# Row maxima out of PSUM by one ScalarE copy, split by ScalarE and GpSimd; bias and residual added by GpSimd

## The chip, the cores and the metric

The kernel runs on one core of one Trainium2 chip. The metric is the device time of one execution in microseconds (us); lower is better. A core has five engines that work side by side, each through its own instruction queue in order: TensorE (PE, with its weight loads shown as PEld), VectorE (DVE), ScalarE (ACT), GpSimd (POOL) and SyncE (SP), which here issues the DMAs. SBUF is the working memory with 128 partitions, PSUM holds the results of TensorE.

## The reference

For x of 2048 tokens and 640 channels:

```python
xn = layernorm(x)
qkv = xn @ wqkv                                  # 32 heads of 20 channels
scores = q @ k.T * 20 ** -0.5                    # each query sees itself and the 255 tokens before it
p = softmax(where(mask, scores, -1e9))
s = (p @ v, heads joined) @ wo
h = relu(xn @ w1 + b1) ** 2                      # 640 -> 1536
g = silu(h @ w2 + b2)                            # 1536 -> 640
return x + s * g
```

## The kernel before

All in 32-bit floats, but TensorE gets most operands as a sum of a rounded high part and a low part (the difference), and adds the products of the parts. Work on the two halves of the 128 partitions (64 rows each) is issued in pairs.

The kernel has three stages. A start normalises x, transposes it and computes values and the first queries and keys. The main loop runs over 16 pairs of heads with 16 blocks of 128 tokens each, one block a step (`for s in range(steps)`, L1165), and fills TensorE in between with the other query and key projections (`qkps`) and the dense branch (`hps`, `yps`). The end transposes the attention's output (`otp`), multiplies it by `wo` (`wops`), and puts gate and residual to it. The order of instructions on every engine is written out by the program: it keeps a planner's clock in `clock[0]`, `fill(upto)` emits filling matmuls until the clock has come to the given time, and `later(wait, fn)` puts a function on a list that `soon` runs once the clock has gone `wait` further. `post` collects DMAs, which `post_all` issues on SP in the order posted.

The softmax needs the maximum of each row before the exponential, but the exponential is taken on transposed scores, where rows lie along the columns. So there are two passes over the scores. At step s, `scores` (L479) computes a block of rows into `sps` (L487), and `maxima` (L491) lets VectorE add the mask and take the row maxima (L495), each into its column of the tile `mt`. After every fourth block, at s % 4 == 0, `max_rows` (L497) transposes `mt` on TensorE (L502), which gives eight rows (2 heads, 4 blocks) of 128 maxima. They go into columns 384 to 447 of the tile that the transposed scores of the same step use. `rest` has ScalarE write the negated high part into `mrow` (L510), and `lows` has VectorE write the low part (L513), both reading the maxima in PSUM. Then four small DMAs (posted in L517, issued in L614) put the rows into the query tile `qs`, as two further rows of the contraction beside its 60. Nine steps after a block of rows, `scores_t` (L527) computes the transposed scores `stps` (L534) for a block of keys, from keys and queries with these two rows, so that they come out with the maxima subtracted. `exps` (L538) has ScalarE take the exponential (L540) into `p32`, and GpSimd zero what is outside the window (L541, L543). A step later ScalarE makes the half-precision high part (`high`, L548), VectorE then the low part (`low`, L554). `values` (L561) multiplies both with the values, `normed` (L587) copies the result out of PSUM (L590), adds its parts and divides on GpSimd (L596 to L600).

The block of keys at step s needs the maxima of three blocks of rows, the last of which is block s - 7 of the pair; the rows posted at a step with s % 4 == 0 are first read three steps later.

What matters for order:

- `pair_tile` (L524) comes from a pool of one buffer: the next step's L534 can write only when all readers of the tile are done, the exponential L540 and, in every fourth step, the readers of the maxima.
- In the loop body, `max_rows` emits the transposes after `scores_t`, then `maxima` follows; `rest` is put off by 1.0 of the planner's clock, and `lows` by another 0.5 from there. So the exponential, and work of other jobs, comes before L510 on ScalarE.
- `mt` is one tile: 32 * (g % 2) picks the columns of a group of four blocks, so successive groups write to different columns, and their rows in PSUM and in `mrow` lie on partitions 0 to 7 and 32 to 39 in turn.
- `mrow` is one buffer, read by the DMAs.

In the end stage, `transposes(u)` (L1080) handles 256 tokens: VectorE adds the bias `b2t` to the dense branch's output `yb` (L1082), then comes the transposition of the attention's output with its split (`split`: ScalarE L108, VectorE L109). ScalarE applies silu (L1112). For each of two token blocks and two halves of the columns, 15 matmuls make `wops`, and `evac` (L1132) lets VectorE multiply it with the gate (L1133) and add the residual (L1134), before the result is stored.

Of the kernel before, what the change touches and what calls it, by code (L numbers as in the profile page):

```python
# [9 lines left out]
F32 = mybir.dt.float32  # L10
F32R = mybir.dt.float32r
BF16 = mybir.dt.bfloat16
F16 = mybir.dt.float16
AF = mybir.ActivationFunctionType
ALU = mybir.AluOpType

P = 128
S = 2048
D = 640
# [10 lines left out]
KR = NPART * DH  # L30
HP = P // 2
# [22 lines left out]
def f32(ap):  # L54
    return ap.bitcast(F32)
# [3 lines left out]
def attn_mlp_kernel(ctx: ExitStack, tc, x, wqkv, wo, w1, b1, w2, b2, out):  # L59
    nc = tc.nc  # L60
    PSUM = bass.MemoryType.PSUM
    const = ctx.enter_context(tc.tile_pool(name="const", bufs=1))
# [26 lines left out]
    ident = const.tile([P, P], F32, name="ident")  # L89
# [4 lines left out]

    nc.gpsimd.affine_select(mask[:, 0:P], mask[:, 0:P], pattern=[[1, P]], compare_op=ALU.is_gt, fill=NEG, base=0, channel_multiplier=-1)
    nc.gpsimd.affine_select(mask[:, 2 * P:], mask[:, 2 * P:], pattern=[[-1, P]], compare_op=ALU.is_ge, fill=NEG, base=0, channel_multiplier=1)
    mt = const.tile([P, P], F32, name="mt")
    nc.gpsimd.memset(mt, 0.0)
    ones = const.tile([2, P], F32, name="ones")
    nc.gpsimd.memset(ones, 1.0)  # L100
    ebias = const.tile([P, 1], F32, name="ebias")
# [389 lines left out]
    def maxima(p, q, ss, nk):  # L491
        for hh in range(2):
            junk = at2.tile([P, 3 * P], BF16, tag="junk", bufs=1, name="junk")
            m = 32 * (q // 4 % 2) + 4 * hh + q % 4
            nc.vector.tensor_tensor_reduce(out=junk[:, :nk], in0=ss[hh][:, :nk], in1=mask[:, 3 * P - nk:], scale=1.0, scalar=-3.0e38, op0=ALU.add, op1=ALU.max, accum_out=mt[:, m:m + 1])  # L495

    def max_rows(p, g, tps):  # L497
        i = p % 2

        def one(j):  # L500
            r = slice(j * HP, (j + 1) * HP)
            nc.tensor.transpose(tps[:, j, 3 * P:3 * P + HP], mt[r, :], ident[r, r])  # L502
        both(lambda: one(0), lambda: one(1), COST[P])

        def rest():
            m = slice(32 * (g % 2), 32 * (g % 2) + 8)
            mrow = at2.tile([40, 2, P], F32R, tag="mrow", bufs=1, name="mrow")[m]
            hi, lo = (mrow[:, a, :].rearrange("m (j n) -> m j n", j=2) for a in range(2))
            src = tps[m, :, 3 * P:3 * P + HP]
            nc.scalar.activation(hi, src, AF.Copy, scale=-1.0)  # L510

            def lows():
                nc.vector.scalar_tensor_tensor(lo, src, -1.0, f32(hi), ALU.mult, ALU.subtract)  # L513
                for hh in range(2):
                    for a in range(2):
                        o = hh * HP + KR + a
                        post(f32(qs[i])[o:o + 1, g * 512:(g + 1) * 512].rearrange("r (q n) -> r q n", q=4), f32(mrow)[4 * hh:4 * hh + 4, a, :])  # L517
            later(0.5, lows)
        return rest

    pts = {}
# [87 lines left out]
    def post(dst, src):  # L609
        posts.append((dst, src))  # L610
# [14 lines left out]
    def later(wait, fn):  # L625
        tasks.append((clock[0] + wait, len(tasks), fn))
# [444 lines left out]
    def out_filler(wo_part):  # L1071
        oT, xts = {}, {}
        b2t = wgt.tile([P, D], F32, tag="wgkl", name="b2t")
        nc.sync.dma_start(b2t, b2.partition_broadcast(P))

        def load_res(t):
            xts[t] = wgt.tile([P, D], F32, tag="wgkh", name="xres")
            nc.sync.dma_start(xts[t], x[t * P:(t + 1) * P, :])

        def transposes(u):  # L1080
            ob, yb = ld[u]
            nc.vector.tensor_add(yb, yb, b2t.unsqueeze(1).to_broadcast([P, 2, D]))  # L1082
            big = bigp.tile([P, KC * BT], F32R, tag="big", name=f"oT_{u}")
            oT[u] = big.rearrange("p (s c n) -> p s c n", s=2, c=KC)
            for c0 in range(0, KC, 2):
                cs = range(c0, min(c0 + 2, KC))
                flush(mark() - 2)
                if state[2] < 10 ** 6:
                    ps = mm_bank([P, len(cs), MT], "otp")
                else:  # L1090
                    ps = pat.tile([P, len(cs), MT], F32, tag="s", name="otp")
                for c in cs:
                    for t in range(2):
                        nc.tensor.transpose(ps[:, c - c0, t * P:(t + 1) * P], ob[:, t, c * P:(c + 1) * P], ident)
                        yield 0.12

                def evac(ps=ps, c0=c0, n=len(cs)):
                    split(oT[u][:, 0, c0:c0 + n], oT[u][:, 1, c0:c0 + n], ps)
                pending.append(evac)

        load_res(0)
        for u in range(2 * NB):
            while u not in ld:
                load(u)
                if u not in ld:
                    yield None
            load(u + 1)
            if u not in oT:
                yield from transposes(u)
            flush()  # L1110
            yb = ld[u][1]
            nc.scalar.activation(yb, yb, AF.Silu)  # L1112
            for t2 in range(2):
                t = 2 * u + t2
                xt = xts.pop(t)
                res = wgt.tile([P, D], F32, tag="wgqh", name="res")
                for nh in range(2):
                    if t2 and not nh and u + 1 in ld:
                        yield from transposes(u + 1)
                    sl = slice(nh * HALF, (nh + 1) * HALF)  # L1120
                    ps = mm_bank([P, HALF], "wops")
                    mms = []
                    for c in range(KC):
                        for op, wp in ((0, 0), (0, 1), (1, 0)):
                            mms.append((oT[u][:, op, c, t2 * P:(t2 + 1) * P], wo_part(wp, c)[:, sl]))
                    yield from mm_group(ps, mms, 0.133)
                    if nh == 0 and t + 1 < NT:
                        load_res(t + 1)
                    load(u + 1)
                    load(u + 2)  # L1130

                    def evac(ps=ps, sl=sl, t2=t2, nh=nh, res=res, xt=xt, t=t, yb=yb):  # L1132
                        nc.vector.tensor_mul(res[:, sl], ps, yb[:, t2, sl])  # L1133
                        nc.vector.tensor_add(res[:, sl], res[:, sl], xt[:, sl])  # L1134
                        if t == NT - 1:
                            post(out[t * P:(t + 1) * P, sl], res[:, sl])
                        elif nh:
                            post(out[t * P:(t + 1) * P, :], res)
                    pending.append(evac)
# [18 lines left out]
    with tc.manual_schedule(engines={E_.PE, E_.Activation, E_.DVE, E_.Pool, E_.SP}):  # L1158
# [6 lines left out]
        for s in range(steps):  # L1165
            state[2] = s
            vload[0] = 0.2 * (s % 4 == 0) + 0.5 * (s % 4 == 3)
            post_all()
            issue(RATE)
            a, b, c, d, e = (at_step(s - lag) for lag in (0, LAG, LAG + 1, LAG + 2, LAG + 3))  # L1170
            if a:
                p, q = a
                if q == 0:
                    ensure_bulk(loads)
                if s == 2:
                    ones_rows(1)
                if q == 2 and p < NP - 1:
                    loads = [bulk_dma(0.7, *l) for l in pair_loads(p + 1, 0)]
                if q == LAG and p < NP - 1:
                    loads += [bulk_dma(0.7, *l) for l in pair_loads(p + 1, 1)]  # L1180
                if q == LAG + 4 and p < NP - 1:
                    load_v(p + 1)
            rows = None
            if a:
                sc = scores(p, q)
            if b:
                stp = scores_t(*b)
            if s % 4 == 0 and 0 < s <= NP * NT:
                rows = max_rows((s - 1) // NT, (s - 1) % NT // 4, stp[0] if b else pair_tile())
            if a:  # L1190
                maxima(*a, *sc)
            if rows:
                later(1.0, rows)
            if norm:
                norm.pop()()
            if b:
                exs[b] = (exps(*b, *stp), stp[1])
            fill((s + EARLY_FILL) * pace)
            drain(urgent)
            if summed:  # L1200
                norm.append(normed(*summed.popleft()))
            post_all()
            issue(RATE)
            if d:
                low(*d)
            flush()
            tick()
            if c:
                high(*c, *exs.pop(c))
            while lastn:  # L1210
                lastn.pop()()
            if e and e[1] % 2:
                fill((s + 1) * pace - 24 * COST[61])
                values(*e)
            else:
                fill((s + 1) * pace)
# [37 lines left out]
```

## Time and profile before

| | |
|---|---|
| median of 3 runs | 985.9 us (984.94 to 987.88) |
| the profiled execution, its time | 987.44 us |
| its span, first to last instruction | 985.4 us |
| mean granted TensorE clock | 0.983 |
| first and last transposes of maxima (L502) | 126.8 and 849.7 us |
| transposes of maxima / copies L510 / subtractions L513 | 128 / 64 / 64 |
| bias additions L1082 on VectorE | 8, 1485 ns each |
| residual additions L1134 on VectorE | 32, 492 ns each |

A row of the profile's timeline has the start, the duration, the engine, the line of the kernel, the operation, what is written from what, the tile's partitions and columns, and the number of instructions merged in the row; in brackets the idle time of the engine before it, with the engine and line that ended it. A row of the waits has the waiting engine and line, what it waited for, the total in us, how often, and the longest. A row of the groups has the count, the busy total in us and the mean of one in ns, and then the engine's idle time before them. All names are the program's own.

### The profile page before, as it was taken

The page shows a single profiled execution, that of the slowest core. Times are in us where ns is not written, and L with a number is a line of the kernel's source. Part 1 is how long each engine was busy: PE and PEld are TensorE (multiplying, and loading weights), DVE is VectorE, ACT ScalarE, POOL GpSimd, SP SyncE. Part 2 cuts the span into 40 slices and gives each one's busy share as a digit, 9 for nine tenths or more (in the row PEclk, how much of TensorE's full clock was granted, in tenths as well). Part 3 has the DMA queues.
Part 4 walks back from the last instruction along what each step waited for, and adds up shares of the span by engine and source line. Part 5 has one row for each costly group of instructions (what it writes and reads, how often), then busy time and mean ns, then how long its engine had stood idle before and what let it go on. Part 6 is the DMA issues. An engine that isn't in the chain of part 4 may idle for free.

```text
span 985.4 us, 35528 instructions
## 1 busy us (share of the span) xinstructions
PE 900.9 (91%) x14368; PEld 862.4 (88%) x14368; DVE 752.1 (76%) x1869; ACT 637.1 (65%) x1080; POOL 501.8 (51%) x798
## 2 busy tenths in 40 slices
PE   9999998999898899899999789898899899898898
PEld 8999998888888899798898788798889789897887
DVE  6864478788999878678888788788688778755664
ACT  5433247686788878678878778767757767852221
POOL 5010015454567767667757657657656676850000
PEclk9999999999999999999999999999999999999999
DMA  7996787578784543452553354463454273065663
GB/s 264 313 382 248 216 279 253 189 227 251 218 258 120 163 120 93 131 153 65 164 145 93 83 149 124 115 194 100 124 156 125 49 230 107 11 201 190 246 242 108
DMA packets 106876, 169.95 MB, mean 172 GB/s; under 512 B 42840, under 2 KB 60376, under 8 KB 104152
## 3 DMA queue, kind: packets, MB, share of 16 engines
q1 hardware_dynamic: 106712, 167.68, 54.3%
q8 instruction: 113, 1.85, 0.8%
q14 instruction: 51, 0.42, 0.2%
HBM read 96.15 MB, written 70.91 MB: 170 GB/s over the span
## 4 chain that ended last, share of the span: by engine, by line
PE 61%; ACT 13%; DVE 11%; DMA 8%; issue 5%; SPq 1%; DVEq 0%; ACTq 0%; POOL 0%; POOLq 0%
PE yps L477 11%; PE hps L477 8%; PE ops L477 8%; PE wops L649 7%; PE vps L228 7%; PE qkps L477 6%; PE stps L534 5%; ACT ph L548 4%; PE sps L487 3%; ACT p L540 3%; PE qkps L205 3%; DVE junk L495 2%; DVE mrow L513 2%; DVE pl L554 2%; ACT relu L959 2%
## 5 line engine op out<-in xcount | busy, mean ns | idle before, releaser
L495 DVE CUSTOM_DVE_ANT_0 junk<-sps,mask 128x384 bf16<-128x384 f32 (+2 forms) x512 | 271.3, 530 | 97.8 <-PE sps L487 47.0
L540 ACT ACTIVATE p<-stps,ebias 128x768 f32<-128x768 f32 (+2 forms) x256 | 219.9, 859 | 158.0 <-PE stps L534 126.9
L541 POOL TENSOR_SCALAR_AFFINE_SELECT p<-p 128x256 f32<-128x256 f32 x256 | 165.1, 645 | 269.8 <-ACT p L540 227.1
L477 PE MATMUL yps<-w,hh 64*128 64x320 f32 x1536 | 260.4, 319 | 6.1 <-DVE sq L964 5.8
L554 DVE TENSOR_TENSOR pl<-p,ph 128x768 f16<-128x768 f32 (+2 forms) x256 | 248.4, 971 | 1.9 <-ACT ph L548 1.5
L477 PE MATMUL hps<-xb,w 64*128 64x256 f32 x2520 | 236.9, 289 | 0.1
L477 PEld LDWEIGHTS hps<-xb,w 64*128 64x128 f32 x2520 | 224.9, 191 | 0.3 <-DVE sq L964 0.3
L477 PEld LDWEIGHTS yps<-w,hh 64*128 64x128 f32 x1536 | 201.3, 189 | 9.5 <-DVE sq L964 8.9
L477 PE MATMUL ops<-vp,ph 64*128 64x61 bf16 x2880 | 205.5, 191 | 0.1
L548 ACT ACTIVATE ph<-p 128x768 f16<-128x768 f32 (+2 forms) x256 | 203.6, 795 | 1.8 <-POOL p L543 1.8
L477 PE MATMUL ops<-vp,pl 64*128 64x61 bf16 x2880 | 203.0, 190 | 0.0
L477 PE MATMUL yps<-w,hl 64*128 64x320 f32 x768 | 192.6, 316 | 0.0
L477 PEld LDWEIGHTS <-ph 64*128 64x128 f16 x2880 | 178.0, 95 | 3.8 <-PE ops L477 0.3
L477 PEld LDWEIGHTS <-pl 64*128 64x128 f16 x2880 | 179.1, 95 | 0.0
L534 PE MATMUL stps<-qs,ks 62*128 62x384 f32 (+2 forms) x512 | 107.9, 360 | 60.7 <-DVE mrow L513 60.3
L543 POOL TENSOR_SCALAR_AFFINE_SELECT p<-p 128x256 f32<-128x256 f32 x224 | 136.0, 607 | 0.0
L534 PEld LDWEIGHTS stps<-qs,ks 62*128 62x128 f32 x512 | 62.8, 190 | 78.1 <-DVE mrow L513 77.8
L477 PEld LDWEIGHTS yps<-w,hl 64*128 64x128 f32 x768 | 122.7, 188 | 0.0
L487 PE MATMUL sps<-ks,qs 60*128 60x384 f32 (+2 forms) x512 | 115.7, 357 | 0.8 <-DVE mt L495 0.7
L477 PE MATMUL qkps<-xT,wgkh 64*128 64x512 f32 x320 | 103.9, 402 | 0.0
L477 PE MATMUL qkps<-xT,wgqh 64*128 64x512 f32 x320 | 103.2, 398 | 0.0
L965 POOL TENSOR_TENSOR hl<-sq,hh 128x256 fp32r<-128x256 f32 x96 | 83.6, 877 | 17.0 <-DVE sq L964 14.2
(109 smaller groups left out, 1622.3 us busy)
## 6 DMA issues: line engine op xcount, KB each, us to landing
ks<-k_d SPq DMA_DIRECT2D x64, 240.0 KB
qs<-q_d SPq DMA_DIRECT2D x64, 240.0 KB
xb<-xs SPq DMA_DIRECT2D x12, 1280.0 KB
xs<-xT SPq DMA_DIRECT2D x8, 1280.0 KB
y<-ysb SPq DMA_DIRECT2D x32, 320.0 KB
k_d<-shm SPq DMA_DIRECT2D x19, 512.0 KB
q_d<-shm SPq DMA_DIRECT2D x19, 512.0 KB
v_d<-vt SPq DMA_DIRECT2D x8, 976.0 KB
```

The lines of the kernel that those rows point to most:

```text
L228: nc.tensor.matmul(ps, xT[xp][b][:, c * BT + t * P: c * BT + (t + 1) * P], wv[wp][:, c, nh * HALF:(nh + 1) * HALF], start=first and m == 0 ...
L477: return nc.tensor.matmul(out, a[r], b_[r], skip_group_check=True, **kw)
L487: nc.tensor.matmul(ss[hh][:, :nk], qs[i][o, q * P:(q + 1) * P], ks[i][o, k0 * P:k0 * P + nk], start=True, stop=True)
L495: nc.vector.tensor_tensor_reduce(out=junk[:, :nk], in0=ss[hh][:, :nk], in1=mask[:, 3 * P - nk:], scale=1.0, scalar=-3.0e38, op0=ALU.add, o ...
L534: nc.tensor.matmul(tps[:, hh, :n], ks[i][o, kb * P:(kb + 1) * P], qs[i][o, kb * P:kb * P + n], start=True, stop=True)
L540: nc.scalar.activation(p32[:, :, :n], tps[:, :, :n], AF.Exp, scale=SCALE, bias=ebias)
L541: nc.gpsimd.affine_select(p32[:, :, 0:P], p32[:, :, 0:P], pattern=[[0, 2], [1, P]], compare_op=ALU.is_ge, fill=0.0, base=0, channel_multip ...
L543: nc.gpsimd.affine_select(p32[:, :, 2 * P:], p32[:, :, 2 * P:], pattern=[[0, 2], [-1, P]], compare_op=ALU.is_gt, fill=0.0, base=0, channel ...
L548: nc.scalar.activation(ph[:, :, :n], p32[:, :, :n], AF.Copy)
L554: nc.vector.tensor_sub(pl[:, :, :n], p32[:, :, :n], ph[:, :, :n])
L649: nc.tensor.matmul(ps, a, b_, start=j == 0, stop=j == n - 1)
L965: nc.gpsimd.tensor_sub(hh[1][:, sl], sq, f32(hh[0][:, sl]))
```

## The change

The single tile for the maxima becomes two tiles of 64 columns, used by successive groups. The transposes therefore give 64 rows, of which the first eight hold the maxima, always on partitions 0 to 7. One ScalarE copy takes the negated maxima out of PSUM into `row` in SBUF. From there ScalarE writes the high part into `mrow`, and GpSimd subtracts to get the low part. All this is no longer put off by the planner's clock: it is emitted right behind the step's exponential, and the exponential now stands ahead of `norm.pop()`. In the end stage, the additions of bias and residual move from VectorE to GpSimd.

```diff
-    mt = const.tile([P, P], F32, name="mt")
-    nc.gpsimd.memset(mt, 0.0)
+    mts = [const.tile([P, HP], F32, name=f"mt{j}") for j in range(2)]
+    for t_ in mts:
+        nc.gpsimd.memset(t_, 0.0)
...
     def maxima(p, q, ss, nk):
         for hh in range(2):
             junk = at2.tile([P, 3 * P], BF16, tag="junk", bufs=1, name="junk")
-            m = 32 * (q // 4 % 2) + 4 * hh + q % 4
-            nc.vector.tensor_tensor_reduce(out=junk[:, :nk], in0=ss[hh][:, :nk], in1=mask[:, 3 * P - nk:], scale=1.0, scalar=-3.0e38, op0=ALU.add, op1=ALU.max, accum_out=mt[:, m:m + 1])
+            m = 4 * hh + q % 4
+            nc.vector.tensor_tensor_reduce(out=junk[:, :nk], in0=ss[hh][:, :nk], in1=mask[:, 3 * P - nk:], scale=1.0, scalar=-3.0e38, op0=ALU.add, op1=ALU.max, accum_out=mts[q // 4 % 2][:, m:m + 1])
 
     def max_rows(p, g, tps):
         i = p % 2
 
         def one(j):
             r = slice(j * HP, (j + 1) * HP)
-            nc.tensor.transpose(tps[:, j, 3 * P:3 * P + HP], mt[r, :], ident[r, r])
+            nc.tensor.transpose(tps[:HP, j, 3 * P:3 * P + HP], mts[g % 2][r, :], ident[r, r])
         both(lambda: one(0), lambda: one(1), COST[P])
 
         def rest():
-            m = slice(32 * (g % 2), 32 * (g % 2) + 8)
-            mrow = at2.tile([40, 2, P], F32R, tag="mrow", bufs=1, name="mrow")[m]
-            hi, lo = (mrow[:, a, :].rearrange("m (j n) -> m j n", j=2) for a in range(2))
-            src = tps[m, :, 3 * P:3 * P + HP]
-            nc.scalar.activation(hi, src, AF.Copy, scale=-1.0)
-
-            def lows():
-                nc.vector.scalar_tensor_tensor(lo, src, -1.0, f32(hi), ALU.mult, ALU.subtract)
-                for hh in range(2):
-                    for a in range(2):
-                        o = hh * HP + KR + a
-                        post(f32(qs[i])[o:o + 1, g * 512:(g + 1) * 512].rearrange("r (q n) -> r q n", q=4), f32(mrow)[4 * hh:4 * hh + 4, a, :])
-            later(0.5, lows)
+            row = at2.tile([8, P], F32, tag="row", bufs=1, name="row")
+            mrow = at2.tile([8, 2, P], F32R, tag="mrow", bufs=1, name="mrow")
+            nc.scalar.activation(row.rearrange("m (j n) -> m j n", j=2), tps[:8, :, 3 * P:3 * P + HP], AF.Copy, scale=-1.0)
+            nc.scalar.activation(mrow[:, 0, :], row, AF.Copy)
+            nc.gpsimd.tensor_sub(mrow[:, 1, :], row, f32(mrow[:, 0, :]))
+            for hh in range(2):
+                for a in range(2):
+                    o = hh * HP + KR + a
+                    post(f32(qs[i])[o:o + 1, g * 512:(g + 1) * 512].rearrange("r (q n) -> r q n", q=4), f32(mrow)[4 * hh:4 * hh + 4, a, :])
         return rest
...
-            nc.vector.tensor_add(yb, yb, b2t.unsqueeze(1).to_broadcast([P, 2, D]))
+            nc.gpsimd.tensor_add(yb, yb, b2t.unsqueeze(1).to_broadcast([P, 2, D]))
...
                         nc.vector.tensor_mul(res[:, sl], ps, yb[:, t2, sl])
-                        nc.vector.tensor_add(res[:, sl], res[:, sl], xt[:, sl])
+                        nc.gpsimd.tensor_add(res[:, sl], res[:, sl], xt[:, sl])
...
             if a:
                 maxima(*a, *sc)
+            if b:
+                exs[b] = (exps(*b, *stp), stp[1])
             if rows:
-                later(1.0, rows)
+                rows()
             if norm:
                 norm.pop()()
-            if b:
-                exs[b] = (exps(*b, *stp), stp[1])
             fill((s + EARLY_FILL) * pace)
```

## The prediction

> **What bounds the kernel now.** The view of engine totals came first, then the list of waits.
>
> ```profile
> span 985.4 us, 35528 instructions
> PE 900.9 (91%) x14368; PEld 862.4 (88%) x14368; DVE 752.1 (76%) x1869; ACT 637.1 (65%) x1080; POOL 501.8 (51%) x798
> ...
> PEld stps L534 <- DVE mrow L513: 77.8, 62, 2.6
> PE stps L534 <- DVE mrow L513: 60.3, 58, 2.4
> ...
> DVE junk L495 <- PE stps L502: 15.2, 35, 1.4
> DVE mrow L513 <- ACT mrow L510: 22.5, 27, 2.2
> ```
>
> TensorE is idle for 985.4 - 900.9 = 84.5 us, and 60.3 us of that is one wait: the transposed scores (L534) cannot be written until VectorE's L513 has read the maxima out of the same, only, `st` tile. It comes 58 times, 60.3 / 58 = 1.04 us each, once in four steps. The weight loads show 77.8 us for it, since they run ahead. I next looked at one such step on ScalarE and VectorE.
>
> ```profile
> 372.75 0.90 ACT L540 ACTIVATE p<-stps,ebias 128x768 f32<-128x768 f32 x1 [0.81 <-PE stps L502]
> 373.55 0.57 ACT L590 ACTIVATE osb<-ops 128x488 f32<-128x488 f32 x1
> 374.01 0.84 ACT L548 ACTIVATE ph<-p 128x768 f16<-128x768 f32 x1
> 374.74 0.25 ACT L510 ACTIVATE mrow<-stps 8x128 fp32r<-8x128 f32 x1
> 375.84 0.90 ACT L540 ACTIVATE p<-stps,ebias 128x768 f32<-128x768 f32 x1 [0.85 <-PE stps L534]
> ...
> 375.02 0.28 DVE L513 SCALAR_TENSOR_TENSOR mrow<-stps,mrow 8x128 fp32r<-8x128 f32 x1
> ```
>
> The exponential ends at 373.65, yet the tile comes free only at 375.30, because L510 is emitted late and stands behind two other ScalarE operations, and L513 follows it. Nothing about the data needs this delay: the transposes were done before the exponential began (its own wait names L502).
>
> The windows of the attention stretch show what the other engines would have to do in less time (columns: length, then busy time of PE, PEld, DVE, ACT, POOL, then the granted clock).
>
> ```profile
> 130.00:200.00 70.00, 65.91 (x898) 62.34 (x896) 57.16 (x149) 46.33 (x70) 30.68 (x54) 0.98 0.70 233
> 200.00:300.00 100.00, 91.47 (x1546) 85.39 (x1544) 89.88 (x225) 75.98 (x117) 55.90 (x93) 1.00 0.78 242
> 300.00:400.00 100.00, 90.84 (x1839) 87.11 (x1836) 84.61 (x220) 81.28 (x142) 72.50 (x113) 1.00 0.41 116
> 400.00:500.00 100.00, 91.70 (x1827) 87.73 (x1822) 78.77 (x209) 76.21 (x133) 67.39 (x108) 0.98 0.43 131
> 500.00:600.00 100.00, 89.43 (x1794) 86.36 (x1795) 80.58 (x212) 77.36 (x131) 65.35 (x103) 0.98 0.44 117
> 600.00:700.00 100.00, 88.58 (x1759) 84.64 (x1756) 83.32 (x216) 75.49 (x127) 68.56 (x107) 0.97 0.46 131
> 700.00:800.00 100.00, 88.69 (x1658) 85.18 (x1660) 76.28 (x204) 67.86 (x115) 63.26 (x104) 0.93 0.46 134
> ```
>
> **The change part by part.** The profiled execution took 987.44 us (2.0 us lie around its span); the median of the runs is 985.9, so its sum stands 1.5 us high. That is left as it is.
>
> *The stall.* After the change one ScalarE copy follows the exponential at once, and its end frees the tile. In the step above that is 373.65 + 0.27 = 373.9 in place of 375.3, and the next L534, with its stall of about a microsecond gone, would come near 374.3. So the wait goes: -60.3 us (the 77.8 us of the weight loads is the outer bound).
>
> *Clock.* The granted clock was below 1 in these windows by 70 x 0.02 + 100 x (0.02 + 0.02 + 0.03 + 0.07) = 15.4 us of full clock. It falls right behind long stalls:
>
> ```profile
> 411.55 0.63 PE L534 MATMUL stps<-qs,ks 62*128 62x384 f32 x2 [1.99 <-DVE mrow L513]
> 412.50:416.00 3.50, 3.50 (x52) 3.50 (x50) 1.00 (x5) 1.25 (x3) 1.34 (x3) 0.61 0.35 77
> 701.50:705.00 3.50, 3.50 (x53) 3.50 (x51) 2.04 (x7) 1.90 (x3) 2.07 (x4) 0.56 0.28 51
> ```
>
> A 1.99 us stall is followed by 3.5 us at 0.61 although TensorE is busy throughout. Between 0 and -15.4 I take -10, since most such windows follow a stall of this line. The Trainium skill, TensorE: Matmul & The Clock Gate (Part 1), says the clock halves after an idle window of about 3.4 us; here it does so after less, and by that rule alone the change would recover nothing, which leaves the sum at -44 in place of -54.
>
> *ScalarE.* L510 (0.25 us) becomes two copies; the second waits for the first, so about 0.3 us more in each of 64 groups, 19 us in all. It lies beside TensorE: per 100 us the stall gives back 60.3 / 740 x 100 = 8.1 us, and in the fullest window ScalarE would have 81.28 + 8.6 x 0.3 = 83.9 us of work in 91.9. Behind the copies in its queue stand `osb`, `ph` and the next exponential, which loses its idle 0.85 us. Without cover it would cost all 19 us.
>
> *VectorE.* It loses L513 (64 x 0.28 = 18 us), its waits for L510 (22.5 us) and, as each group has its own `mts` tile, the waits of the maxima for the transposes (15.2 us). In the window with 89.88 us it has 87.5 us to do in 91.9: full, but below TensorE. For lag on ScalarE and VectorE together I take +6 us, between 0 (the totals fit) and +30 (half of the stall returns).
>
> *GpSimd and the row DMAs.* The subtraction has no row of its own; the nearest are these.
>
> ```profile
> L600 POOL TENSOR_TENSOR on<-on,rs 128x160 f32<-128x160 f32 x64 | 31.1, 486 | 0.2
> L965 POOL TENSOR_TENSOR hl<-sq,hh 128x256 fp32r<-128x256 f32 x96 | 83.6, 877 | 17.0 <-DVE sq L964 14.2 <-ACT hh L960 1.2 <-PE stps L534 0.9
> L184 POOL TENSOR_TENSOR wv<-wvr,wv 128x640 fp32r<-128x640 f32 x5 | 7.7, 1572 | 0.0
> ...
> 652.88 0.90 ACT L540 ACTIVATE p<-stps,ebias 128x768 f32<-128x768 f32 x1 [0.86 <-PE stps L502]
> 654.20 1.12 POOL L543 TENSOR_SCALAR_AFFINE_SELECT p<-p 128x256 f32<-128x256 f32 x1
> 656.75 2.51 SPq L614 DMA_DIRECT2D qs<-mrow  x4
> 660.64 0.34 PE L534 MATMUL stps<-qs,ks 62*128 62x384 f32 x1
> ```
>
> Its row has 128 columns, so 0.49 us at most, and I take that. It queues behind the two selections of its step, which end 655.32 - 652.88 = 2.44 us after the exponential's start. The four DMAs take 2.51 us on SP as now; this group, with the smallest gap of those I compared, needed no wait although L534 came 660.64 - 659.26 = 1.38 us after the last issue, so landing takes 1.38 at most. The chain is then 2.44 + 0.49 + 2.51 + 1.38 = 6.8 us. L534 needs the rows three steps later. The 256 exponentials run from 139.5 to 873.0, 2.88 us a step, 2.64 without the stall:
>
> ```profile
> L540 ACT ACTIVATE p<-stps,ebias x256: 457/902/922, 139.5 to 873.0; 128x768 f32<-128x768 f32 x112, 128x512 f32<-128x512 f32 x16
> ```
>
> So the rows are due 3 x 2.64 - 0.55 = 7.4 us after that start (0.55 from L534 to its exponential). It fits by 0.6 us: priced at nothing; behind these DMAs on SP stand prefetches and stores. The single `mrow` buffer must be empty by the next group, 4 x 2.64 = 10.6 us later: covered.
>
> *The transposes.* Their weights shrink from 64x128 to 64x64. If the array then works in another tiling, it changes twice a group. Two changes between other tilings in this trace show
>
> ```profile
> 116.47 0.19 PEld L487 LDWEIGHTS sps<-ks,qs 60*128 60x128 f32 x2 [0.19 <-issue]
> 888.29 0.85 PEld L1094 LDWEIGHTS otp<-ident,ob 128*128 128x128 f32 x8 [0.19 <-DMA y<-ysb]
> ```
>
> 0.19 us of idle weight loading each. The bounds are 0 and 2 x 64 x 0.19 = 24 us; I take the middle, +12. The Trainium skill, TensorEngine Tiling (Key Properties), states that a change of tiling mode drains the engine; by it the term is the full 24 and the sum -42.
>
> *The end of the kernel.* VectorE waits for the bias `b2t`, and TensorE for VectorE:
>
> ```profile
> 888.99 1.09 ACT L108 ACTIVATE oT<-otp 128x512 fp32r<-128x512 f32 x2 [5.61 <-PE otp L1094]
> 890.82 1.49 DVE L1082 TENSOR_TENSOR yb<-yb,b2t 128x1280 f32<-128x1280 f32 x1 [1.93 <-DMA b2t<-in_B_b_dram]
> 892.23 1.28 DVE L109 TENSOR_TENSOR oT<-otp,oT 128x512 fp32r<-128x512 f32 x2
> 892.97 0.65 PE L1094 MATMUL otp<-ident,ob 128*128 128x128 f32 x2 [3.58 <-DVE oT L109]
> ...
> 982.11 0.49 DVE L1134 TENSOR_TENSOR res<-res,xres 128x320 f32<-128x320 f32 x1
> ```
>
> With the addition on GpSimd, L109 starts behind ScalarE's first copy, at 889.6 in place of 892.23: -2.6 us. GpSimd's rates, (1572 - 877) / 384 = 1.8 ns a column, make its 1280 columns 2.7 us, done near 893.6; the first product then waits in one of three banks while TensorE fills the others. Eight such additions and 32 residual additions of 1.0 us are 54 us in 95, all of it cover but the last: it adds 1.0 - 0.49 = +0.5 us after L1133.
>
> Sum: -60.3 - 10 + 6 + 12 - 2.6 + 0.5 = -54.4, so 987.4 - 54.4 = **933 us**.
>
> **The rivals.** *A. The tiling drains in full and no clock returns*: -60.3 + 6 + 24 - 2.6 + 0.5 = -32.4, 955 us. For it: the idle 0.19; against it: the clock drops behind these stalls. *B. The wait moves*: ScalarE or VectorE is late, or the rows land late, for half of the stall (+30 in place of +6): 957 us. For it: VectorE at 89.88 of 100, and 0.6 us to spare on the rows; against it: every total fits. *C. Slower*: GpSimd works in order, so the subtraction stands behind whatever it finds. If two additions and an `hl` are ahead (some 2 us in all: 0.49 twice, 0.88), the chain is 8.7 us against 7.4, and L534 waits 1.3 us on a DMA each time: 933 + 62 x 1.3 = 1014. The tipping point is 7.4 + 54.4 / 62 = 8.3 us. For it: one unit of order for all; against it: GpSimd is 72.50 of 100 busy at most, and the selections run as soon as the exponential is done. *D. It doesn't do what it says*: the copy waits on ScalarE for something as late as before, 986 us; against it stands the exponential's own wait for L502.
>
> **How the numbers follow.** Forecast 0.62, A 0.12, B 0.13, C 0.10, D 0.03. Within 0.3% (3 us) is about what a measurement can't tell from no change: faster 0.87, same 0.03, slower 0.10. The forecast's own ends: no tiling cost and all of the clock, 987.4 - 60.3 - 15.4 - 2.1 + 6 = 916, and the weight loads' 17.5 us beyond it, 898; on the other side B with its rows, 957, and a little more. I take 902 to 964.
>
> **What would show it.** Right: no wait of L534 for `mrow` or for the copy; a granted clock near 1.00 from 400 to 800; steps of about 2.7 us throughout; L109 near 0.6 us after ScalarE's first copy at the end. Wrong: L534 or its weight load waiting for `qs<-mrow` DMAs (B, C), for ScalarE's copy (D), idle on "issue" around the transposes (A); maxima late for the scores (L487).

## The result and the profile after

The changed kernel takes 925.3 us (924.86 to 925.4, 4 runs) against 986.3 us, a ratio of 0.938 with a 95% interval of 0.9364 to 0.9397. The forecast was 933 us, range 902 to 964. The profiled execution went from 987.44 to 925.29 us, its span from 985.4 to 923.6 us.

First the engine totals of the kernel after, and then its waits of TensorE. The line numbers have moved: L531 is the old L534, L496 the old L495, L488 the old L487, L961 the old L964; L509 is the new copy out of PSUM, L510 the high part, L511 GpSimd's low part.

```profile
span 923.6 us, 35641 instructions
PE 887.2 (96%) x14368; PEld 853.6 (92%) x14368; DVE 712.2 (77%) x1765; ACT 647.2 (70%) x1144; POOL 583.8 (63%) x903
```

```profile
PE yps L478 <- DVE sq L961: 12.0, 17, 1.4
PE otp L1091 <- DVE oT L110: 8.0, 8, 1.0
PE sps L488 <- DVE mt L496: 4.8, 17, 0.6
PE stps L531 <- DMA qs<-mrow: 1.9, 1, 1.9
PE hps L478 <- DVE sq L961: 1.2, 3, 0.5
PE stps L531 <- ACT p L537: 0.5, 2, 0.2
PE stps L531 <- ACT row L509: 0.4, 2, 0.2
```

The wait of 60.3 us has left 2.8 us at the same line, of which ScalarE's copy holds 0.4. The 61.8 us by which the span fell can be told in two parts. TensorE's idle time fell from 84.5 to 36.4 us (48.1), its busy time from 900.9 to 887.2 us (13.7), with the same 14368 matmuls. The busy time fell with the clock: (1 - 0.983) x 985.4 = 16.8 us were lost to it before, (1 - 0.998) x 923.6 = 1.8 us after. New idle time took a part back: waits of `yps` for L961 went from 5.8 to 12.0 us, the maxima L496 from 0.7 to 4.8 us. The two rows of the kernel before:

```profile
PE yps L477 <- DVE sq L964: 5.8, 7, 1.2
PE sps L487 <- DVE mt L495: 0.7, 3, 0.3
```

The timeline of one row step, ScalarE and then GpSimd:

```profile
367.62 0.89 ACT L537 ACTIVATE p<-stps,ebias 128x768 f32<-128x768 f32 x1
368.41 0.25 ACT L509 ACTIVATE row<-stps 8x128 f32<-8x128 f32 x1
368.69 0.31 ACT L510 ACTIVATE mrow<-row 8x128 fp32r<-8x128 f32 x1
368.90 0.55 ACT L587 ACTIVATE osb<-ops 128x488 f32<-128x488 f32 x1
369.36 0.83 ACT L545 ACTIVATE ph<-p 128x768 f16<-128x768 f32 x1
370.10 0.88 ACT L537 ACTIVATE p<-stps,ebias 128x768 f32<-128x768 f32 x1
...
368.94 0.41 POOL L540 TENSOR_SCALAR_AFFINE_SELECT p<-p 128x256 f32<-128x256 f32 x1
369.32 0.45 POOL L511 TENSOR_TENSOR mrow<-row,mrow 8x128 fp32r<-8x128 f32 x1
```

The tile is free at 368.66, 1.04 us after the exponential's start (2.55 in the step shown before), and the next exponential starts 2.48 us after this one, where it was 3.09. In this step ScalarE goes from one exponential to the next with no idle time, so a longer copy would delay the second one. L511 starts when the selections are done and waits for nothing.

The windows after, in the columns of those before:

```profile
200.00:300.00 100.00, 98.14 (x1684) 91.86 (x1683) 93.57 (x228) 83.81 (x138) 67.60 (x111) 1.00 0.79 247
400.00:500.00 100.00, 98.31 (x2060) 96.81 (x2057) 84.53 (x224) 85.67 (x152) 80.06 (x128) 1.00 0.45 134
500.00:600.00 100.00, 92.70 (x1814) 87.36 (x1809) 87.92 (x217) 87.82 (x159) 76.57 (x124) 1.00 0.44 118
600.00:700.00 100.00, 97.97 (x1984) 95.26 (x1983) 89.24 (x235) 78.16 (x134) 76.30 (x125) 1.00 0.57 168
```

In three of these windows TensorE is busy 98 of 100 us, where the windows before had 88.6 to 91.7, and at full clock. It isn't so everywhere: 500 to 600 has 92.7, and there TensorE waits 4.1 us for the squares and 2.4 us for the maxima; 300 to 400 has 96.25, and 700 to 800 has 95.78 at a clock of 0.98. VectorE is at 93.6 in the first window shown.

### The profile page after: what moved, and what is told of

Read it like the earlier page. It is cut to its first block, busy times and chain, and to the rows that moved or that the text cites. A ratio compares the mean times of both kernels' runs of the same rounds, so it can differ in the third digit from the quotient of the medians.

```text
span 923.6 us, 35641 instructions
## 1 busy us (share of the span) xinstructions
PE 887.2 (96%) x14368; PEld 853.6 (92%) x14368; DVE 712.2 (77%) x1765; ACT 647.2 (70%) x1144; POOL 583.8 (63%) x903
## 4 chain that ended last, share of the span: by engine, by line
PE 70%; DVE 12%; ACT 7%; issue 7%; DMA 2%; POOL 1%; DVEq 0%; POOLq 0%; ACTq 0%; SPq 0%
PE yps L478 15%; PE ops L478 10%; PE hps L478 10%; PE qkps L478 8%; PE vps L229 8%; PE wops L646 7%; PE sps L488 4%; DVE junk L496 4%; PE stps L531 3%; PE qkps L206 3%; DVE pl L551 2%; DVE sq L961 2%; ACT p L537 2%; ACT ph L545 2%; ACT relu L956 1%
## 5 line engine op out<-in xcount | busy, mean ns | idle before, releaser
L496 DVE CUSTOM_DVE_ANT_0 junk<-sps,mask 128x384 bf16<-128x384 f32 (+2 forms) x512 | 270.6, 528 | 74.4 <-PE sps L488 31.6
L551 DVE TENSOR_TENSOR pl<-p,ph 128x768 f16<-128x768 f32 (+2 forms) x256 | 256.5, 1003 | 2.2 <-ACT ph L545 1.8
L478 PEld LDWEIGHTS hps<-xb,w 64*128 64x128 f32 x2520 | 219.4, 186 | 2.9 <-DVE sq L961 2.7
L478 PEld LDWEIGHTS yps<-w,hh 64*128 64x128 f32 x1536 | 196.8, 185 | 17.7 <-DVE sq L961 17.1
L478 PE MATMUL ops<-vp,ph 64*128 64x61 bf16 x2880 | 201.5, 189 | 0.1
L478 PE MATMUL yps<-w,hl 64*128 64x320 f32 x768 | 188.5, 313 | 0.0
L478 PEld LDWEIGHTS <-ph 64*128 64x128 f16 x2880 | 174.3, 94 | 3.9 <-PE sps L488 0.7
L478 PEld LDWEIGHTS <-pl 64*128 64x128 f16 x2880 | 175.4, 94 | 0.2 <-DVE pl L551 0.2
L488 PE MATMUL sps<-ks,qs 60*128 60x384 f32 (+2 forms) x512 | 121.9, 357 | 5.2 <-DVE mt L496 4.8
L478 PEld LDWEIGHTS yps<-w,hl 64*128 64x128 f32 x768 | 119.0, 185 | 0.0
L531 PE MATMUL stps<-qs,ks 62*128 62x384 f32 (+2 forms) x512 | 109.2, 341 | 2.9 <-DMA qs<-mrow 1.9
L488 PEld LDWEIGHTS sps<-ks,qs 60*128 60x128 f32 x512 | 69.0, 186 | 13.9 <-DVE mt L496 13.2
```

The source lines that it names most:

```text
L478: return nc.tensor.matmul(out, a[r], b_[r], skip_group_check=True, **kw)
L488: nc.tensor.matmul(ss[hh][:, :nk], qs[i][o, q * P:(q + 1) * P], ks[i][o, k0 * P:k0 * P + nk], start=True, stop=True)
L531: nc.tensor.matmul(tps[:, hh, :n], ks[i][o, kb * P:(kb + 1) * P], qs[i][o, kb * P:kb * P + n], start=True, stop=True)
L551: nc.vector.tensor_sub(pl[:, :, :n], p32[:, :, :n], ph[:, :, :n])
```

## The experiments

The experiments ran in four sessions on four chips. The mark is the changed kernel itself, run again in one of them (beside e8 and e9), so most comparisons with it go across chips. The kernel before ran in all four, with medians of 988.3 to 989.6 us and single runs from 984.9 to 993.9, so differences of two or three us are not told apart by medians.

**The changed kernel again**

> The changed kernel itself, on the chip of these runs, as the mark for them: 922 to 928 us. Either a profile with one late landing of the row DMAs near 750 us (about 3 us) or one without.

922.8 us (921.6 to 925.3). Its profile has a span of 919.9 us, 3.7 us less than the one above. The windows of both explain it, the one above first, then this one:

```profile
742.00:746.00 4.00, 4.00 (x74) 3.95 (x71) 3.73 (x10) 2.96 (x4) 3.36 (x7) 1.00 0.95 358
746.00:750.00 4.00, 2.06 (x23) 1.61 (x20) 2.90 (x7) 0.95 (x2) 1.22 (x2) 1.00 0.88 300
750.00:754.00 4.00, 4.00 (x77) 4.00 (x75) 1.90 (x6) 2.16 (x5) 1.31 (x3) 0.57 0.06 16
```

```profile
742.00:746.00 4.00, 4.00 (x76) 3.99 (x73) 3.71 (x12) 3.18 (x5) 3.35 (x7) 1.00 0.93 332
746.00:750.00 4.00, 4.00 (x93) 3.78 (x90) 3.71 (x12) 2.17 (x3) 2.92 (x4) 1.00 0.73 284
750.00:754.00 4.00, 4.00 (x78) 4.00 (x75) 3.40 (x9) 3.53 (x7) 2.89 (x5) 1.00 0.15 32
```

In the first, L531 stood 1.94 us for the row DMAs while the DMA engines moved 300 to 358 GB/s; TensorE was idle for 1.94 of four us, and the next four ran at a clock of 0.57. In the second neither happens, though its DMA engines were nearly as busy (332 and 284 GB/s). The rows are that close to late; what made them late in the one and not in the other is not shown.

**The place alone, from both sides**

The first takes the early place out of the changed kernel, the second puts it alone into the kernel before. Both move the exponential and the copies together; which of the two moves counts is not separated.

```diff
@@ e1: the changed kernel
-            if b:
-                exs[b] = (exps(*b, *stp), stp[1])
             if rows:
-                rows()
+                later(1.0, rows)
             if norm:
                 norm.pop()()
+            if b:
+                exs[b] = (exps(*b, *stp), stp[1])
@@ e2: the kernel before
+            if b:
+                exs[b] = (exps(*b, *stp), stp[1])
             if rows:
-                later(1.0, rows)
+                rows()
             if norm:
                 norm.pop()()
-            if b:
-                exs[b] = (exps(*b, *stp), stp[1])
...
-            later(0.5, lows)
+            lows()
```

> The changed kernel with the old places in the loop: the copy put off by 1.0 of the planner's clock, the exponential behind norm. Theory (the place of the copy sets when the tile is free): the copy starts 1.1 us or more behind the exponential again, VectorE's part of the old wait (about 0.6 us) stays away, so TensorE waits some 0.4 us for it in each of 62 steps, now on ScalarE's copy: 25 to 35 us slower than the changed kernel, 950 to 960 us, and part of the clock loss returns. Rival (the single reader and the relief of VectorE are what counts): within 5 us of the changed kernel, 925 to 930 us.

> The kernel before with nothing changed but the places: the high copy right behind the exponential, the low part on VectorE at once behind the two maxima of its step, both still read PSUM; the old maxima tile and the old end stay. Theory (place): most of the wait of L534 goes, 5 to 15 us of it stay as VectorE reads last; with the old end 930 to 945 us. Rival (one reader is needed): 960 us or more.

With the late place: 950.1 us (949.5 to 951.8), 27 us above the mark, and 39 us below the kernel before. Half of the old wait is back, on ScalarE's copy, and the clock fell to 0.992; this row is from its waits:

```profile
PE stps L531 <- ACT row L509: 29.8, 31, 2.0
```

With the early place alone: 941.6 us (939.4 to 944.2), 47 us below the kernel before. Its waits:

```profile
PE yps L477 <- DVE sq L964: 16.3, 17, 1.8
DVE mrow L513 <- ACT mrow L510: 14.8, 21, 1.8
PE hps L477 <- DVE sq L964: 7.1, 8, 2.3
PE stps L534 <- DVE mrow L513: 0.2, 1, 0.2
```

So the early place alone brings 47 us of the 66 between the kernel before and the mark, and everything but the early place brings 39. The two add up to more than the whole, since either one shortens the same wait: without VectorE as a reader it falls from 60.3 to 29.8 us, with the early place to almost nothing. One reader is not needed to free the tile: the wait for L513 is 0.2 us where I had expected 5 to 15.

What the early place alone lacks against the mark stands elsewhere. TensorE waits 23.4 us for the squares in the two lines, against 13.0 us in the mark and 5.8 in the kernel before (its only such line with more than a trace). The clock is 0.989, and TensorE's busy time 896.3 us against 885.0 in the mark. So the clock can stay low with the wait for L513 gone. Behind the late squares there may be VectorE's 14.8 us of standing still in front of L513, but it stood there for 22.5 us in the kernel before, when TensorE was slower; that the standing still is the cause is shown only by the next three kernels, and there in part.

**VectorE in place of GpSimd, at three places**

```diff
@@ e6: low part on VectorE, at the same place
-            nc.gpsimd.tensor_sub(mrow[:, 1, :], row, f32(mrow[:, 0, :]))
+            nc.vector.tensor_sub(mrow[:, 1, :], row, f32(mrow[:, 0, :]))
@@ e8: the same, with the four posts in lows()
+            later(0.5, lows)
@@ e10: lows() kept in a list lw, and in the loop
             if d:
                 low(*d)
+            while lw:
+                lw.pop()()
+                post_all()
```

> The changed kernel with the low part computed on VectorE, from the SBUF row. Theory (off the path, since the tile is free already): 0 to 3 us slower, 925 to 928 us, with VectorE 18 us busier. Rival (VectorE is so full that only GpSimd could take it): 6 us or more slower, with longer waits of TensorE for L496 and L961.

> The low part on VectorE as in the run with 948 us, but put off by 0.5 of the planner's clock behind the copies, so that other VectorE work comes first. Theory (there VectorE stood still in order until ScalarE's copy was done, 25.6 us in 38 waits, and what is behind it came late): most of the 23 us return, 925 to 932 us, and VectorE's wait for L510 falls under 8 us. Rival (VectorE's load of 18 to 29 us is what costs): 940 us or more.

> The low part on VectorE, placed behind the step's L551 in the loop, so that ScalarE's copies are long done. It separates VectorE's load from its waiting. If waiting alone cost the time (25.6 us of it went with 26 us, 14.2 us with 15 us), VectorE's wait for L510 is below 4 us and the time 923 to 928 us. If the load of some 25 us costs too, 932 us or more though the wait is gone. In both cases rows that land late would show as waits of L531 for DMAs.

At the same place: 948.5 us (946.3 to 950.4), 25.7 above the mark, a miss: I had expected 0 to 3. It is slower even than the early place alone with two readers of PSUM (941.6 us): there VectorE has one ScalarE copy to wait for, here two, and it waits 25.6 us against 14.8. The timeline of VectorE in that kernel shows the wait.

```profile
374.24 0.08 DVE L496 DVE_READ_ACCUMULATOR2_ANT mt<- 128x1 f32 x1
375.94 0.45 DVE L511 TENSOR_TENSOR mrow<-row,mrow 8x128 fp32r<-8x128 f32 x1 [1.62 <-ACT mrow L510]
376.33 0.47 DVE L961 SCALAR_TENSOR_TENSOR sq<-hps,b1t,relu 128x256 f32<-128x256 f32 x1
376.72 0.94 DVE L551 TENSOR_TENSOR pl<-p,ph 128x768 f16<-128x768 f32 x1
```

L511 reads SBUF and holds no tile of TensorE's, yet VectorE stands 1.62 us in front of it until ScalarE has written the high part, with the squares and L551 behind. Later places: 937.6 us (932.8 to 941.2) with `later(0.5)`, 935.3 us (930.1 to 937.5) behind L551. The rows of the waits, of the three kernels in this order (in the last two the row step's L531 has another number):

```profile
DVE mrow L511 <- ACT mrow L510: 25.6, 38, 2.1
PE yps L478 <- DVE sq L961: 18.4, 20, 2.4
PE hps L478 <- DVE sq L961: 9.7, 10, 2.8
PE stps L531 <- DMA qs<-mrow: 0.6, 1, 0.6
```

```profile
DVE mrow L513 <- ACT mrow L510: 14.2, 23, 1.2
PE yps L478 <- DVE sq L964: 15.4, 20, 1.5
PE hps L478 <- DVE sq L964: 2.4, 5, 0.8
PE stps L534 <- DMA qs<-mrow: 4.8, 3, 1.9
```

```profile
DVE mrow L513 <- ACT mrow L510: 0.6, 2, 0.3
PE yps L478 <- DVE sq L965: 15.7, 19, 1.5
PE hps L478 <- DVE sq L965: 2.2, 5, 0.7
PE stps L535 <- DMA qs<-mrow: 4.6, 4, 1.9
```

VectorE's standing still goes from 25.6 to 14.2 to 0.6 us, and 10.9 and then 13.2 of the 25.7 us come back, about half. The first was expected at 925 to 932 us with a wait below 8 us, and missed both. For the second I had written that 932 us or more with the wait gone would mean that VectorE's load costs too, and it came out so. What stays in the profiles of the two late places is 4.6 to 4.8 us of waiting for rows that land late, a clock of 0.992 and 0.994 against 1.000 for the mark (7.5 and 5.6 us of clock), and some 5 us of waiting for the squares above the mark's 11.9 and 1.1. The late rows and the clock are not all of it: the fastest runs of the two kernels had clocks of 1.000 and 0.999 and still took 932.8 and 930.1 us. How much of the rest is VectorE's 25 to 27 us in this line was not separated. None of the three places tried is good for this subtraction on VectorE: early it stands still, late the rows are late. GpSimd has one, since it is busy with the selections just while ScalarE copies.

**The end of the kernel**

```diff
@@ e3: bias and residual back on VectorE (e4: the residual alone)
-            nc.gpsimd.tensor_add(yb, yb, b2t.unsqueeze(1).to_broadcast([P, 2, D]))
+            nc.vector.tensor_add(yb, yb, b2t.unsqueeze(1).to_broadcast([P, 2, D]))
...
-                        nc.gpsimd.tensor_add(res[:, sl], res[:, sl], xt[:, sl])
+                        nc.vector.tensor_add(res[:, sl], res[:, sl], xt[:, sl])
```

> The changed kernel with bias and residual back on VectorE. Theory (the wait for the bias at the start of the end stage held VectorE and TensorE): 2 to 4 us slower than the changed kernel, 927 to 929 us. Rival (the end stage's edits are worth nothing, or cost): 925 us or less.

> The changed kernel with only the residual back on VectorE, the bias stays on GpSimd. Theory (the residual on GpSimd brings nothing and its last addition costs 0.4 us): 924.5 to 925 us. Rival (VectorE is relieved by it where TensorE waits): 926 us or more.

Old end: 925.4 us (924.7 to 930.2), 2.6 above the mark, as expected in size but within the spread; its profile shows the wait itself, 10.4 us with a longest of 3.5 for the split against 8.0 and 1.0. The clock fell at that place as well:

```profile
836.00:840.00 4.00, 3.92 (x17) 3.92 (x18) 2.44 (x4) 2.94 (x3) 0.00 (x0) 0.57 0.89 337
```

Residual alone: 927.5 us (922.6 to 931.7), not told apart from anything; its profile has 920.9 us against 919.9.

**The transposes and the two tiles**

```diff
@@ e5: weights of 80 columns
-    mts = [const.tile([P, HP], F32, name=f"mt{j}") for j in range(2)]
+    mts = [const.tile([P, 80], F32, name=f"mt{j}") for j in range(2)]
...
-            nc.tensor.transpose(tps[:HP, j, 3 * P:3 * P + HP], mts[g % 2][r, :], ident[r, r])
+            nc.tensor.transpose(tps[:80, j, 3 * P:3 * P + HP], mts[g % 2][r, :], ident[r, r])
@@ e7: one tile
+    mts = [const.tile([P, HP], F32, name="mt0")] * 2
```

> The changed kernel with maxima tiles of 80 columns, so that the transposes' weights are 64x80 and not 64x64. Theory (the smaller tiling costs nothing here): within 1 us of the changed kernel. Rival (each change of tiling drains the array, 0.1 to 0.19 us twice a group): 12 to 24 us faster, 901 to 913 us.

> The changed kernel with one maxima tile of 64 columns for all groups, so that the maxima of a group wait for the transposes of the one before, as in the kernel before. Theory (VectorE's 15 us of waits for the transposes lie beside TensorE): 0 to 3 us slower. Rival (VectorE's lag then reaches TensorE): 5 to 15 us slower, 930 to 940 us.

923.2 us (922.1 to 926.9) and 922.4 us (921.4 to 927.8): both are the mark's. The smaller weights cost nothing that can be seen, which the weight loads show too (start, duration), of the kernel before and then of the changed kernel:

```profile
372.08 0.24 PEld L534 LDWEIGHTS stps<-qs,ks 62*128 62x128 f32 x2
372.25 0.19 PEld L502 LDWEIGHTS stps<-ident,mt 64*128 64x128 f32 x2
372.43 0.10 PEld L477 LDWEIGHTS <-ph 64*128 64x128 f16 x1
```

```profile
335.72 0.20 PEld L531 LDWEIGHTS stps<-qs,ks 62*128 62x128 f32 x2
335.90 0.12 PEld L503 LDWEIGHTS stps<-ident,mt 64*64 64x64 f32 x2
336.07 0.09 PEld L478 LDWEIGHTS <-ph 64*128 64x128 f16 x1
```

In the changed kernel a tile of 64*64 stands between one of 62*128 and one of 64*128, and each load starts 0.17 to 0.18 us after the one before, as in the kernel before, where that tile is 64*128. The kernel with 80 columns shows 64*80 for its transposes; whether the array works in another tiling in any of the three is not shown. With one maxima tile VectorE waits 12.7 us for the transposes again, beside TensorE, so the second tile brings no time.

**What is left: the place of the squares**

The squares' `later(0.7, rest)` in the first layer became 0.4 in one kernel and 0.9 in another.

> The changed kernel with VectorE's squares (L961) put off by 0.4 of the planner's clock and not 0.7. Theory (what is left of TensorE's waiting, 12 us for L961, is again a matter of place in VectorE's queue): 4 to 10 us faster than the changed kernel, with that wait below 6 us. Rival (VectorE then waits for ScalarE's relu in order, as it did for the copies): no gain, or up to 10 us slower.

> The changed kernel with VectorE's squares put off by 0.9 of the planner's clock and not 0.7, the other side of the run with 0.4, which was 12 us slower. If the place chosen already balances VectorE's standing still against TensorE's wait for the bank: 0 to 10 us slower. If sooner was wrong because VectorE waited for relu, and that wait (9.2 us) still counts: 2 to 6 us faster.

934.6 us (932.5 to 935.7) and 938.0 us (937.4 to 938.6), both slower than the mark, by 12 and 15 us, and by more than either of the two outcomes written down for each. Sooner, VectorE's wait for the relu rose from 9.2 to 15.6 us and TensorE's for the maxima from 4.6 to 9.9, while its wait of `yps` for the squares fell only from 11.9 to 10.4. But most of the 14.0 us between the two spans is not that: TensorE waited 3.7 us for late rows and was busy for 892.6 us in place of 885.0, at a clock of 0.992. So what the sooner place does by itself is not separated from late rows and clock. Later, VectorE's wait for the relu rose to 33.3 us as well, and TensorE's for the squares from 11.9 to 21.0 (`yps`) and from 1.1 to 7.7 (`hps`). Of these three places 0.7 is the best. No kernel tried was clearly faster than the changed one.

## Why the prediction was right

The direction, the mechanism and the range held: 925.3 us against 933, with the time 7.7 us better than the sum. That the sum came so near is in part luck: the terms for the clock and the tiling made it 17 us too slow, those for the stall and the lag 8 us too fast. By its steps, against the profile:

- *The stall*, -60.3: gone but for 2.8 us, and the exponentials come every (815.6 - 139.3) / 255 = 2.65 us, as forecast. The early place alone takes the wait for L513 to 0.2 us; without the early place 29.8 us of it return.
- *Clock*, -10: the loss over the whole span fell by 15.0 us. In the windows of the bound it fell from 15.4 to 2.0 us (a clock of 0.98 from 700 to 800); the rest lay at the end, where the kernel before had 0.97 from 850 to 900, around the stall of 3.58 us that the move of the bias shortens. In the second profile of the changed kernel it is at 1.000 with no such stall left; in the first, one stall of 1.94 us came back, and the clock fell to 0.57 behind it. The Trainium skill, TensorE: Matmul & The Clock Gate (Part 1), has idleness halve the clock, which these rows agree with; that two us of it suffice is from the rows alone. Which waits the clock falls behind was not settled: it was 0.989 in the kernel with the early place alone, where TensorE's waiting is for the squares.
- *ScalarE*, 19 us beside TensorE: 36 us of copies replace 16.6 us, 19 us more, and TensorE waits 0.9 us in all for ScalarE at L531.
- *Lag*, +6: mis-sized. TensorE's waits for the squares and the maxima rose by 6.2 + 4.1 us in the main lines and 1.2 us for the first layer, 11.5 us. VectorE was fuller still than the window of 89.88 us had shown, 93.57 of 100, and its L551 even got slower, from 971 to 1003 ns in the mean. The waits for the transposes that the second tile spares VectorE brought nothing: with one tile the time is the mark's.
- *The tiling*, +12: the step that failed. I priced a switch by two idle times of weight loads next to other tilings (0.19 us), one of which the profile puts down to a DMA, `y<-ysb`. Between 64*128 and 64*64 no such time is there: the loads are 0.17 to 0.18 us apart in both kernels, and 80 columns change nothing. The drain that the Trainium skill names (TensorEngine Tiling, Key Properties) is not seen here.
- *GpSimd and the rows*, nothing: the subtraction takes 0.57 us in the mean, not 0.49 at most, and once in the first profile the rows were late, since landing can take longer than the 1.38 us that I had bounded it by from one group. The slack was small.
- *The end*, -2.6 + 0.5: the first `wops` comes 832.57 - 830.31 = 2.26 us after the first transposition, where it was 4.98; the split starts 831.63 - 831.00 = 0.63 us behind ScalarE's first copy, as forecast; the last addition takes 0.86 us and not 0.49.

Rival B came true in small (lag and one late landing). C did not: L531 waited for the rows once, 1.9 us. What C feared of GpSimd, an operation that stands in order among others, is what befell VectorE in the variants. A and D fell.

With measured sizes the sum is -57.5 (stall, less what stays at L531) - 15.0 + 11.5 - 2.7 + 0.4 = -63.3, against 62.15 us by which the profiled execution fell.

## What to carry to other kernels

Where the bounding engine waits for a buffer, look at where in the reader's queue the read stands as well as at who reads: here the early place alone was worth 47 of some 66 us, and all the rest without it 39. An operation that waits in an in-order queue holds up all that stands behind it. That costs time where the bounding engine needs what is behind: the subtraction at its early place on VectorE cost 25.7 us, while VectorE's 12.7 us of waiting for the transposes, in the kernel with one maxima tile, cost nothing that can be seen. So give such an operation to an engine that is busy with something else until its input is ready. And stalls of TensorE can cost more than themselves: behind one of 1.94 us the next four us ran at a clock of 0.57.

## What the runs showed of the hardware that was not expected

A stall of TensorE of only 1.94 us, which ended at 748.22, was followed by half the clock, and not at once: windows of a quarter of a us show 1.00 up to 750.00, then 0.50, and 1.00 again from 753.50, some 3.4 us in all. The kernel with 80 columns had no wait for rows; its clock fell to 0.90 from 665 to 670 and 0.76 from 670 to 675, around a wait of 1.39 us for the squares. Not every such stall does it: the kernel before had 58 waits for L513, 1.04 us each, and its loss of 16.8 us makes about ten stretches of 3.4 us at half the clock (an estimate: each loses 1.7 us, and 16.8 / 1.7 = 9.9).

Four DMAs of 2 KB each had landed within 1.38 us of the last issue in one group of the kernel before. In the first profile of the changed kernel they were not there when L531 wanted them 748.22 - 744.04 - 1.94 = 2.24 us after the last issue, and came 1.94 us later, while the engines moved 300 to 358 GB/s. In the second profile, at the same place, they were there 746.25 - 744.25 = 2.0 us after it, with 284 to 332 GB/s. The cause of the difference is open. GpSimd needs 0.57 us in the mean for a subtraction of 8 x 128, VectorE 0.39 to 0.43.
